# Three stretches put in program order, w_out's words kept in PSUM, key and query copies moved from VectorE to ScalarE

## The chip, the cores and the metric

The kernel runs on one NeuronCore of a Trainium2 chip. Its engines are named as the profile names them: PE (TensorE, with PEld its weight loads), DVE (VectorE), ACT (ScalarE), POOL (GpSimd) and SP (SyncE, which here only issues transfers). The metric is the device time of one execution in microseconds (us); the median of three runs is compared.

## The reference

Three layers follow each other on 4 sequences of 576 tokens, 8 heads of 64.

```python
# 1 attention with a decay
scores = q @ k.T / 8 + cum[:, None] - cum[None, :]      # cum = cumsum(log(clip(f)))
x = softmax(causal(scores)) @ v                          # -> x: 2304 tokens x 512
# 2 dense layer
h = x @ w_in                                             # 512 -> 2048
x = (h * clip(h + 3, 0, 6) / 6) @ w_out                  # 2048 -> 512
# 3 eight experts, one per token
e_idx = argmax(x @ w_gate); gate_w = softmax(x @ w_gate)[e_idx]
eom = sigmoid(x @ w_output_gate)[e_idx]
out = gate_w * eom * (relu(x @ w1[e_idx]) @ w2[e_idx])   # 512 -> 1024 -> 512
```

## The kernel before, in words

Every float32 operand is held as two 16-bit parts, a high part (`hi`, float16, written by ACT) and the rest (`lo`, bfloat16, by DVE or POOL), and each product is three matmuls (hi by hi, hi by lo, lo by hi).

**Attention** runs per sequence `b` through units. `("q", b, h, qbs)` is one head's query blocks: `score` (PE line 288, then DVE line 335, which adds the mask and takes the row minimum into `nm`), `soft` (ACT exponential, line 369; then a transpose of the weights, on PE for the first units, by DMA later) and `pv` (PE lines 421 to 423, after every second head DVE lines 444 to 446 into `xs`, ACT 449 and POOL 450 into `xn`). The PSUM tile `pv` has one buffer. `("p", b, n)` prepares a piece of K and Q: the first four pieces by PE transposes (lines 225 to 230), the later ones by DMA transposes, after which DVE copies one half of K into `K2` (line 246) and one half of Q into `Q2` (line 269). `plan` lists the units; for sequence 0 the pieces 2 and 3 stand after `AT2` and `AT3` units of the first group. `decay` computes `cum` on ACT and DVE, `setup` fills masks and constants on POOL.

**The dense layer** works on chunks `c` of 384 tokens. `moe1_steps(c)` does 16 steps of 12 matmuls (line 688), each evacuated by ACT (692), DVE (695), ACT (696) and DVE or POOL (700), with three PSUM buffers `mm`; then four groups of 48 matmuls with w_out (line 711). Chunk c can start when its tokens' `xn` have been transposed by DMA (`xtrans`, line 484, issued by SP).

**Weights of the dense layer** come as 64-bit floats. `conv_raw` turns one piece of 512 words a partition into float32 by three integer operations on DVE (lines 651, 653, 655; the intermediate `tp` is the PSUM tile `cv`, one buffer, the result `t` an SBUF tile `w32`, two buffers), then ACT writes `hi` (658) and POOL (for w_in) or DVE (for w_out) writes `lo` (659). There are 16 pieces of each matrix. w_in is converted before chunk 0, w_out while chunk 0 runs.

**Routing and experts.** `gate_steps` computes the gates of a chunk, `rank_onehot` (931) and `table` (909, 913 to 922) the lists of tokens per expert; `gather` (POOL 943, then a DMA transpose by SP, 946) fetches them. For experts 0 and 1 the first block of tokens (`blocks` (0,)) is taken from the first five chunks alone, gathered into `wi`, and multiplied (`expert1`, line 969, tile `wi`; `expert2`, line 988) before the remaining tokens' tables are needed. Then `round_` does everything else; it begins by loading the counts of the experts into registers of each engine (`values_load`, line 1183, eight TENSOR_LOADs an engine).

**Order.** A scheduler with a model of the engines orders most instructions by priority; inside `tc.manual_schedule(engines=...)` the listed engines keep the program's order. Before, that held for SP during the first part, and for PE, ACT and DVE inside `round_(True)` only. `tc.issue_after(ins)` keeps what is written inside it behind `ins` on that engine.

Of the kernel before, what the change touches and what calls it, by code (L numbers as in the profile page):

```python
# [18 lines left out]
P = 128  # L19
# [17 lines left out]
AT2, AT3 = 0, 4  # L37
# [21 lines left out]
def attention_moe_kernel(ctx: ExitStack, tc: tile.TileContext, q, k, v, f, w_in, w_out,  # L59
# [36 lines left out]
    def setup():  # L96
        nc.gpsimd.memset(ident, 1.0)
        nc.gpsimd.affine_select(out=ident, in_=ident, pattern=[[1, P]], compare_op=ALU.is_equal, fill=0.0, base=0,
                                channel_multiplier=-1)
        nc.gpsimd.memset(mask, 0.0)  # L100
        for c in range(2):
            ms_ = mask[c * 64:c * 64 + 64, 512:640]
            nc.gpsimd.affine_select(out=ms_, in_=ms_, pattern=[[-1, 128]], compare_op=ALU.is_ge, fill=-1e15,
                                    base=c, channel_multiplier=2)
        nc.gpsimd.memset(mask4, 0.0)
        for hf in range(2):
            nc.gpsimd.affine_select(out=mask4[hf * 64:hf * 64 + 64], in_=mask4[hf * 64:hf * 64 + 64],
                                    pattern=[[-1, 64]], compare_op=ALU.is_ge, fill=-1e15, base=0,
                                    channel_multiplier=1)
        nc.gpsimd.memset(bias3, 3.0)  # L110
        for t in Q2:
            nc.gpsimd.memset(t[64:67], PSC)
        for t in vt:
            nc.gpsimd.memset(t[:, :, :, 64:65], 1.0)

            nc.gpsimd.memset(t[64:128, 4, :, 65:129], 0.0)


    cumd = dram.tile([15, B * H, P], F16, name="cumd")

    def decay():
        ft = ap1.tile([P, 576], F32, tag="ms", name="ft", bufs=3)[0:B * H]
# [8 lines left out]
        nc.gpsimd.memset(cpt[:, :, S:640], 0.0)  # L131
        cp = cpt[:, :, 0:S]
# [6 lines left out]
        nc.vector.tensor_tensor(out=cp[:, 2], in0=ones, in1=cp[:, 1], op=ALU.subtract)  # L139
# [78 lines left out]
    def split_transposed(nm, i, hi, lo, copy):  # L218
# [3 lines left out]
        for c in range(2):  # L222
# [7 lines left out]
            nc.gpsimd.tensor_copy(out=copy[c], in_=hi[c])  # L230

    def prep_k(i):
# [13 lines left out]
        nc.vector.tensor_copy(out=k2[0:64], in_=k1[0:64])  # L246

    def prep_q(i):
# [20 lines left out]
        nc.vector.tensor_copy(out=q2[0:64, :, 0:r], in_=q1[64:128, :, 0:r])  # L269
# [280 lines left out]
    def attn_seq():  # L550
# [10 lines left out]
        with tc.high_priority(offset=ATTN_FIRST):  # L561
            cp = decay()
        setup()
        load(0, "kq")
        ahead(0)
        load(1, "kq")
        ahead(1)
        prep_k(0)
        prep_q(0)
        load(0, "v")  # L570
        store_decay(cp)
        ahead(2)
        load(1, "v")
        for hh in range(2):
            load_cum(0, hh)
        prep_k(1)
        prep_q(1)
# [62 lines left out]
    def conv_raw(nm, i):  # L640
# [3 lines left out]
        else:  # L644
# [4 lines left out]
        t = stp.tile([P, WL // 4], I32, tag="w32", name="w32", bufs=2)  # L649
        tp = ps_cv.tile([P, WL // 4], I32, tag="cv", name="cv")  # L650
        nc.vector.tensor_scalar(out=tp, in0=w[:, :, 1], scalar1=3, scalar2=0x3FFFFFFF,
                                op0=ALU.logical_shift_left, op1=ALU.bitwise_and)
        nc.vector.scalar_tensor_tensor(out=tp, in0=w[:, :, 1], scalar=-0x40000000, in1=tp, op0=ALU.bitwise_and,
                                       op1=ALU.bitwise_or)
        nc.vector.scalar_tensor_tensor(out=t, in0=w[:, :, 0], scalar=29, in1=tp, op0=ALU.logical_shift_right,
# [85 lines left out]
    def setup_gates():  # L741
# [5 lines left out]
        nc.gpsimd.memset(allone, 1.0)  # L747
# [263 lines left out]
    def ahead(i):  # L1011
        for _ in range(AHEAD[i]):
            load_next(nc.sync)
# [119 lines left out]
    count_rounds()  # L1133
    for i in range(NBL, NB):
        rank_onehot(R, i, P, CAP)
    table(R, P, const, ps_mm, (1, 2), NB)

    for e in range(2):
        for _ in expert1(e, ps_mm, (0,)):
            pass  # L1140
# [54 lines left out]
    ET = mybir.EngineType  # L1195
    with tc.manual_schedule(engines={ET.PE, ET.Activation, ET.DVE}):
        round_(True)
# [38 lines left out]
```

## Time and profile before

| | us |
|---|---|
| median of 3 runs | 835.37 (833.76 to 836.37) |
| the profiled execution, whole | 831.17 |
| its span, first to last instruction | 829.5 |
| PE busy in it | 746.0 (90%) |
| DVE busy | 486.3 (59%) |
| ACT busy | 427.3 (52%) |
| mean granted TensorE clock | 0.962 |

The profiled execution is 4.2 us (0.5%) below the median of the runs. Durations below come from it; a difference worked out from them is then applied to the median. A busy share is an average over stages that are limited by different engines, so stages are read one by one. [...]

### The profile page before, as it was taken

How to read it: one execution, taken by the hardware profiler on the slowest of the kernel's cores; microseconds unless marked ns; L12 is line 12 of the kernel's file. 1: busy time of each engine (PE TensorE's matmuls, PEld its weight loads, DVE VectorE, ACT ScalarE, POOL GpSimd, SP SyncE). 2: the span in 40 equal slices, each digit the busy share in tenths (PEclk: the TensorE clock that was granted, in tenths of full speed). 3: DMA queues.
4: the chain of work that ended last, by engine and by line, in shares of the span. 5: the costliest groups of instructions: out<-in, count | busy, mean ns of one | idle time of the engine just before them, and what ended most of it. 6: DMA issues, size and time to landing. Idle time of an engine off the chain costs nothing. (4 is left out here: it accounts for less than half of the span.)

```text
span 829.5 us, 16702 instructions
## 1 busy us (share of the span) xinstructions
PE 746.0 (90%) x6166; PEld 480.1 (58%) x6177; DVE 486.3 (59%) x1302; ACT 427.3 (52%) x879; POOL 314.1 (38%) x388
## 2 busy tenths in 40 slices
PE   4745998889899989998999999999889999999993
PEld 2533455545566645665665656666769665667641
DVE  7998999838852865158723777760313555554510
ACT  4864776557754774256733655550113555454510
POOL 9546777656744463256522500000131322210010
PEclk9986999979999999998999999999899999999997
DMA  8758789999995684479623847612463899795410
GB/s 247 218 184 190 173 186 236 214 129 164 174 169 115 137 153 83 72 119 168 109 50 71 144 130 237 187 41 51 78 147 86 249 275 276 221 266 206 149 39 28
DMA packets 263779, 127.96 MB, mean 154 GB/s; under 512 B 214658, under 2 KB 247522, under 8 KB 263684
## 3 DMA queue, kind: packets, MB, share of 16 engines
q1 hardware_dynamic: 251860, 105.20, 58.1%
q0 software_dynamic: 4960, 15.73, 5.6%
q10 hardware_dynamic: 6864, 5.80, 2.5%
q8 instruction: 54, 0.88, 0.5%
q14 instruction: 41, 0.34, 0.2%
HBM read 71.52 MB, written 10.08 MB: 98 GB/s over the span
## 5 line engine op out<-in xcount | busy, mean ns | idle before, releaser
L688 PE MATMUL mm<-xT,wi 128*128 128x384 f16 (+1 forms) x1152 | 211.9, 332 | 9.1 <-DMA xT<-xn 4.9
L711 PE MATMUL mm<-g,wo 128*128 128x384 f16 (+1 forms) x1152 | 201.8, 328 | 0.4 <-DVE hr L695 0.4
L688 PEld LDWEIGHTS <-wi 128*128 128x128 f16 (+1 forms) x1152 | 111.0, 99 | 88.8 <-issue 21.5
L711 PEld LDWEIGHTS <-wo 128*128 128x128 f16 (+1 forms) x1152 | 111.7, 98 | 74.4 <-issue 3.8
L969 PEld LDWEIGHTS <-W 128*128 128x128 f16 (+1 forms) x1344 | 102.8, 101 | 15.2 <-issue 6.8
L369 ACT ACTIVATE ms<-ms,nm 128x512 f32<-128x512 f32 (+4 forms) x144 | 79.5, 579 | 55.5 <-DVE nm L335 30.5
L872 DVE TENSOR_TENSOR W<-stw,W 128x1024 bf16<-128x1024 f32 x64 | 77.7, 1224 | 50.6 <-ACT W L871 50.2
L387 POOL TENSOR_TENSOR pn<-ms,pn 128x384 bf16<-128x384 f32 (+1 forms) x80 | 83.0, 1044 | 62.2 <-ACT pn L386 53.4
L969 PE MATMUL mm<-xs,W 128*128 128x256 f16 (+3 forms) x1152 | 96.8, 246 | 5.9 <-DMA xs<-xg 3.6
L988 PE MATMUL mm<-W,hT 128*128 128x512 f16 (+1 forms) x422 | 93.8, 379 | 1.1
L871 ACT ACTIVATE W<-stw 128x1024 f16<-128x1024 f32 x64 | 66.8, 1054 | 45.4 <-DMA stw<-in_moe_w_dram 42.9
L335 DVE CUSTOM_DVE_ANT_1 ms<-sc,mask 128x128 f32<-128x128 f32 (+3 forms) x128 | 58.9, 485 | 24.6 <-PE sc L288 13.9
L988 PEld LDWEIGHTS <-hT 128*128 128x128 f16 (+1 forms) x432 | 41.9, 98 | 50.9 <-issue 1.6
L696 ACT ACTIVATE g<-hr 128x384 f16<-128x384 f32 x96 | 49.9, 520 | 41.2 <-DVE hr L695 40.6
L700 DVE TENSOR_TENSOR g<-hr,g 128x384 bf16<-128x384 f32 x80 | 53.8, 673 | 25.7 <-ACT g L696 25.5
L695 DVE SCALAR_TENSOR_TENSOR hr<-hr,mm 128x384 f32<-128x384 f32 x96 | 52.6, 548 | 16.1 <-ACT hr L692 15.4
L973 DVE SCALAR_TENSOR_TENSOR hT<-mm,hT 128x128 bf16<-128x128 f32 (+1 forms) x96 | 32.6, 355 | 47.9 <-ACT hT L972 43.3
L288 PE MATMUL sc<-K,q 128*128 128x256 f16 (+3 forms) x192 | 49.1, 300 | 12.8 <-DVE nm L335 9.1
L692 ACT ACTIVATE hr<-mm,bias 128x384 f32<-128x384 f32 x96 | 54.5, 568 | 11.5 <-PE mm L688 10.1
L995 POOL DMA_INDIRECT out_dram<-y,ids x18 | 20.1, 1115 | 96.4 <-ACT y L994 56.1
L421 PE MATMUL pv<-vt,pt 128*128 128x65 f16 x320 | 42.0, 199 | 15.6 <-DVE xs L446 9.5
L943 POOL DMA_INDIRECT xg<-rows,ids x22 | 24.9, 1130 | 70.7 <-DMA xs<-xg 63.7
(186 smaller groups left out, 1128.3 us busy)
## 6 DMA issues: line engine op xcount, KB each, us to landing
stw<-in_moe_w_dram SPq DMA_DIRECT2D x64, 512.0 KB
wo<-in_moe_w_in_dram SPq DMA_DIRECT2D x16, 512.0 KB
raw<-in_moe_w_out_dram ACTq DMA_DIRECT2D x11, 512.0 KB
rows<-rw POOLq DMA_DIRECT2D x15, 256.0 KB, 4.0
ldk<-in_k_dram SPq DMA_DIRECT2D x14, 256.0 KB
ldq<-in_q_dram SPq DMA_DIRECT2D x14, 256.0 KB
ldv<-in_v_dram SPq DMA_DIRECT2D x13, 256.0 KB
g<-in_moe_w_out_dram SPq DMA_DIRECT2D x3, 512.0 KB
```

Of the source, the lines that this page charges most:

```text
L335: nc.vector.tensor_tensor_reduce(out=pairs(ms[:, off:off + w]), in0=ps[:, 0:w].rearrange("p (c j) -> p c j", c=2), in1=pairs(mask[:, 640 - ...
L369: nc.scalar.activation(out=ms[:, off:off + w], in_=ms[:, off:off + w], func=AF.Exp, scale=-1.0, bias=nm[:, i:i + 1])
L387: nc.gpsimd.tensor_tensor(out=lo.bitcast(BF16), in0=ms[:, 0:N], in1=hi, op=ALU.subtract)
L688: nc.tensor.matmul(ps[:, 0:w], lhsT=l.bitcast(BF16) if a else l, rhs=r.bitcast(BF16) if b2 else r, start=i == 0, stop=i == 3 * KD - 1)
L692: nc.scalar.activation(out=hr, in_=ps[:, 0:w], func=AF.Relu, bias=bias3)
L695: nc.vector.scalar_tensor_tensor(out=hr, in0=hr, scalar=6.0, in1=ps[:, 0:w], op0=ALU.min, op1=ALU.mult)
L700: either.tensor_tensor(out=g[:, m, 1, 0:w].bitcast(BF16), in0=hr, in1=g[:, m, 0, 0:w], op=ALU.subtract)
L711: nc.tensor.matmul(ps[:, 0:w], lhsT=l.bitcast(BF16) if a else l, rhs=r.bitcast(BF16) if b2 else r, start=i == 0, stop=i == 3 * NF - 1)
L871: nc.scalar.activation(out=hi, in_=sts[i], func=AF.Copy)
L872: nc.vector.tensor_tensor(out=lo.bitcast(BF16), in0=sts[i], in1=hi, op=ALU.subtract)
L969: nc.tensor.matmul(ps[:, 0:w], lhsT=l.bitcast(BF16) if a else l, rhs=r.bitcast(BF16) if b2 else r, start=i == 0, stop=i == 3 * KD - 1)
L988: nc.tensor.matmul(ps, lhsT=l.bitcast(BF16) if a else l, rhs=r.bitcast(BF16) if b2 else r, start=i == 0, stop=i == 3 * NF2 - 1)
```

## The change

The program's beginning (`decay`, the first loads and pieces 0 and 1) is put in program order on PE, ACT, DVE and POOL; `ident` is made first and the rest of `setup` inside `decay`. The constants for routing are written by POOL only behind the last copy of the split K and Q pieces (`hold[-1]`), and the first conversion of w_in behind the decay's last operation (`hold[0]`). Pieces 2 and 3 of sequence 0 move from places 0 and 4 to 3 and 6. The copies of lines 246 and 269 go from DVE to ACT. For w_out the converted words stay in the PSUM tile `cv`, in place. In routing, two steps of `expert1(0)` are written ahead of the remaining `rank_onehot` and `table`, and from there PE, ACT and DVE keep the program's order up to the end of `round_(True)`.

```diff
-AT2, AT3 = 0, 4
+AT2, AT3 = 3, 6
...
-    def setup():
+    def setup_ident():
         nc.gpsimd.memset(ident, 1.0)
         nc.gpsimd.affine_select(out=ident, in_=ident, pattern=[[1, P]], compare_op=ALU.is_equal, fill=0.0, base=0,
                                 channel_multiplier=-1)
+
+    def setup():
         nc.gpsimd.memset(mask, 0.0)
...
     def decay():
+        setup_ident()
...
         nc.gpsimd.memset(cpt[:, :, S:640], 0.0)
+        setup()
...
-        nc.vector.tensor_tensor(out=cp[:, 2], in0=ones, in1=cp[:, 1], op=ALU.subtract)
+        hold.append(nc.vector.tensor_tensor(out=cp[:, 2], in0=ones, in1=cp[:, 1], op=ALU.subtract).ins)
...
-            nc.gpsimd.tensor_copy(out=copy[c], in_=hi[c])
+            last = nc.gpsimd.tensor_copy(out=copy[c], in_=hi[c])
+        hold.append(last.ins)
...
-        nc.vector.tensor_copy(out=k2[0:64], in_=k1[0:64])
+        nc.scalar.activation(out=k2[0:64], in_=k1[0:64], func=AF.Copy)
...
-        nc.vector.tensor_copy(out=q2[0:64, :, 0:r], in_=q1[64:128, :, 0:r])
+        nc.scalar.activation(out=q2[0:64, :, 0:r], in_=q1[64:128, :, 0:r], func=AF.Copy)
...
-        with tc.high_priority(offset=ATTN_FIRST):
+        ET = mybir.EngineType
+        with tc.manual_schedule(engines={ET.PE, ET.Activation, ET.DVE, ET.Pool}):
             cp = decay()
...
-        t = stp.tile([P, WL // 4], I32, tag="w32", name="w32", bufs=2)
         tp = ps_cv.tile([P, WL // 4], I32, tag="cv", name="cv")
-        nc.vector.tensor_scalar(out=tp, in0=w[:, :, 1], scalar1=3, scalar2=0x3FFFFFFF,
-                                op0=ALU.logical_shift_left, op1=ALU.bitwise_and)
+        with tc.issue_after(hold[0]) if (nm, i) == ("wi", 0) else nullcontext():
+            nc.vector.tensor_scalar(out=tp, in0=w[:, :, 1], scalar1=3, scalar2=0x3FFFFFFF,
+                                    op0=ALU.logical_shift_left, op1=ALU.bitwise_and)
...
+        t = stp.tile([P, WL // 4], I32, tag="w32", name="w32", bufs=2) if nm == "wi" else tp
...
-        nc.gpsimd.memset(allone, 1.0)
+        with tc.issue_after(hold[-1]):
+            nc.gpsimd.memset(allone, 1.0)
+            setup_tables()
...
+    first = [expert1(e, ps_mm, (0,)) for e in range(2)]
+    manual = ctx.enter_context(ExitStack())
+    manual.enter_context(tc.manual_schedule(engines={ET.PE, ET.Activation, ET.DVE}))
+    run(first[0], 2)
     for i in range(NBL, NB):
         rank_onehot(R, i, P, CAP)
     table(R, P, const, ps_mm, (1, 2), NB)
-
-    for e in range(2):
-        for _ in expert1(e, ps_mm, (0,)):
-            pass
+    for g_ in first:
+        run(g_, F2 // P)
...
-    with tc.manual_schedule(engines={ET.PE, ET.Activation, ET.DVE}):
-        round_(True)
+    round_(True)
+    manual.close()
```

What this does to the engines' orders is shown at three places. In the changed program the lines stand 5 to 16 further down (225 is 230, 335 is 341, 651 is 657, 659 is 667, 969 is 981, 972 is 984, 988 is 1000, 994 is 1006, 1183 is 1199).

ACT at the end of the experts' first block; `wi<-mm` are evacuations of `expert1` on that block, `wi<-mm,cf` of its `expert2`, `hT<-mm` those of `round_`. Before:

```order
L972 ACTIVATE wi<-mm 128x128 x15
L1183 TENSOR_LOAD cnt x8
L972 ACTIVATE hT<-mm 128x128
L972 ACTIVATE wi<-mm 128x128
L994 ACTIVATE wi<-mm,cf 128x512 x2
L972 ACTIVATE hT<-mm 128x128 x7
```

And changed:

```order
L984 ACTIVATE wi<-mm 128x128 x16
L1006 ACTIVATE wi<-mm,cf 128x512 x2
L1199 TENSOR_LOAD cnt x8
L984 ACTIVATE hT<-mm 128x128 x8
```

The eight register loads moved from inside the first product of that block to behind its second product.

PE around its eight register loads; `wi` marks the first block, `xs` the tokens that `round_` gathers. Before:

```order
L969 MATMUL mm<-wi,W_7248 128x128
L969 LDWEIGHTS W_7129
L1183 TENSOR_LOAD cnt x8
L969 MATMUL mm<-xs_8461,W_7129 128x128
```

And changed:

```order
L1000 MATMUL mm<-W_7640,wi 128x512
L981 LDWEIGHTS W_7116
L1199 TENSOR_LOAD cnt x8
L981 MATMUL mm<-xs_8448,W_7116 128x128
```

Before, 144 of the 192 matmuls of line 969 on the first block stand ahead of the loads, and behind them the other 48, mixed with twenty on `xs`, and then the 48 of line 988; changed, all 192 and the 48 of line 988 stand ahead of the loads and nothing on `xs` does.

DVE at the very beginning; `ft`, `ones` and `cp` belong to `decay`, lines 651, 653 and 655 to the conversion of w_in, 229 to the split of K and Q. Before:

```order
L136 CAST cp<-ones 32x576
L651 TENSOR_SCALAR cv<-wo 128x512
L137 TENSOR_TENSOR ones<-ones,cp 32x576
L653 SCALAR_TENSOR_TENSOR cv<-wo,cv 128x512
L138 CAST cp<-ones 32x576
L655 SCALAR_TENSOR_TENSOR w_280<-wo,cv 128x512
L139 TENSOR_TENSOR cp<-ones,cp 32x576
L229 TENSOR_TENSOR K_93<-mm,K_93 64x512
```

And changed:

```order
L141 CAST cp<-ones 32x576
L142 TENSOR_TENSOR ones<-ones,cp 32x576
L143 CAST cp<-ones 32x576
L144 TENSOR_TENSOR cp<-ones,cp 32x576
L234 TENSOR_TENSOR K_93<-mm,K_93 64x512 x2
L234 TENSOR_TENSOR q_184<-mm,Q_0_88 64x8x64
L657 TENSOR_SCALAR cv<-wo 128x512
```

The first conversion moved from among the decay's operations to behind the first three splits.

## Rows read from the trace of the kernel before

**Rows 1.** The page: busy time of each engine in the whole span, then the granted TensorE clock in 40 equal slices, in tenths.

```profile
PE 746.0 (90%) x6166; PEld 480.1 (58%) x6177; DVE 486.3 (59%) x1302; ACT 427.3 (52%) x879; POOL 314.1 (38%) x388
PEclk9986999979999999998999999999899999999997
```

**Rows 2.** Stretches of the span (us): their length, then busy us of PE, PEld, DVE, ACT, POOL with their instruction counts, granted clock, DMA share and GB/s.

```profile
0.00:68.00 68.00, 37.65 (x324) 26.66 (x324) 60.80 (x156) 42.69 (x90) 43.31 (x78) 0.89 0.76 219
73.00:160.00 87.00, 76.85 (x583) 46.25 (x583) 81.44 (x189) 59.40 (x125) 63.35 (x65) 0.97 0.93 203
160.00:200.00 40.00, 35.85 (x350) 21.51 (x347) 20.54 (x69) 24.33 (x54) 22.59 (x31) 0.85 0.91 145
200.00:400.00 200.00, 190.10 (x1617) 119.17 (x1614) 119.81 (x401) 117.22 (x266) 99.26 (x121) 0.98 0.73 133
```

**Rows 3.** What PE waited for from 73 to 560 us: us in total, times, longest.

```profile
PE sc L288 <- DVE nm L335: 7.0, 9, 1.3
PE mm L688 <- DVE hr L695: 3.4, 6, 1.0
PE pv L421 <- DVE xs L446: 2.3, 1, 2.3
PE pv L421 <- DVE xs L462: 2.2, 4, 1.3
PE sc L288 <- DMA q<-qp: 1.5, 1, 1.5
```

**Rows 4.** The timeline of the first 24 us: start, us, engine, line, operation, and in brackets the idle time before it and what ended it.

```profile
7.26 2.77 PE L225 MATMUL mm<-ident,g 128*64 128x128 f32 x12 [7.26 <-POOL ident L98]
8.35 0.69 DVE L651 TENSOR_SCALAR cv<-wo 128x512 int32<-128x512 int32 x1 [0.84 <-DMA wo<-in_moe_w_in_dram]
12.02 0.69 DVE L229 TENSOR_TENSOR K<-mm,K 64x512 f16<-64x512 f32 x1
23.04 0.29 DVE L335 CUSTOM_DVE_ANT_1 ms<-sc,mask 128x128 f32<-128x128 f32 x1
```

**Rows 5.** The timeline where the dense layer's first chunk starts: the last evacuation of attention that it needs, its transpose, its first matmuls.

```profile
67.77 0.28 DVE L446 TENSOR_TENSOR xs<-pv,rl 128x128 f32<-128x128 f32 x1
70.17 1.26 SPq L484 DMA_TRANSPOSE xT<-xn  x1
73.37 5.91 PE L688 MATMUL mm<-xT,wi 128*128 128x384 f16 x26 [3.72 <-DMA xT<-xn]
```

**Rows 6.** Durations: the instructions of lines 659 and 246 (ns minimum/median/maximum, first and last start), groups by form (busy us, mean ns), then two stretches with DVE's busy time in line 246 alone and the same two in line 269 alone.

```profile
L659 DVE TENSOR_TENSOR wo<-w,wo x16: 669/778/2959, 80.2 to 158.0; 128x512 bf16<-128x512 f32 x16
L659 DVE TENSOR_TENSOR wo<-w,wo 128x512 bf16<-128x512 f32 x16 | 18.0, 1127 | 0.1
L229 DVE TENSOR_TENSOR K<-mm,K 64x512 f16<-64x512 f32 x8 | 5.5, 682 | 0.3 <-ACT K L228 0.2
L246 DVE COPY K<-K x12: 412/419/1374, 99.3 to 368.7; 64x1024 f16<-64x1024 f16 x12
73.00:160.00 87.00, 4.08 (x6) 0.97 0.93 203
160.00:400.00 240.00, 5.64 (x10) 0.96 0.76 135
73.00:160.00 87.00, 5.23 (x6) 0.97 0.93 203
160.00:400.00 240.00, 5.38 (x10) 0.96 0.76 135
L871 ACT ACTIVATE W<-stw 128x1024 f16<-128x1024 f32 x64 | 66.8, 1054 | 45.4 <-DMA stw<-in_moe_w_dram 42.9 <-SPq L1200 1.9 <-ACTq L1172 0.3
L658 ACT ACTIVATE wo<-w 128x512 f16<-128x512 f32 x16 | 10.0, 624 | 4.6 <-DVE w L655 4.5
```

**Rows 7.** PE's timeline in routing, from the first block's first product to the first product of `round_`.

```profile
593.72 2.74 PE L969 MATMUL mm<-wi,W 128*128 128x128 f16 x24
596.26 1.19 PE L909 MATMUL mm<-M,R 128*128 128x56 bf16 x21
597.26 7.56 PE L969 MATMUL mm<-wi,W 128*128 128x128 f16 x120
608.38 0.72 PE L969 MATMUL mm<-xs,W 128*128 128x128 f16 x10 [3.55 <-DMA xs<-xg]
613.80 10.52 PE L988 MATMUL mm<-W,wi 128*128 128x512 f16 x47
624.16 8.04 PE L969 MATMUL mm<-xs,W 128*128 128x128 f16 x141
```

**Rows 8.** The register loads of line 1183 on PE's and ACT's sequencers (ns minimum/median/maximum, first and last start), and the branch of line 1191 with the matmuls written ahead of it.

```profile
L1183 PEldq TENSOR_LOAD <-cnt x8: 298/314/755, 603.7 to 607.2; - x8
L1183 ACTq TENSOR_LOAD <-cnt x8: 274/285/748, 612.8 to 616.1; - x8
L1191 PEldq COMPARE_BRANCH  x12: 65/172/326, 645.8 to 811.9; - x12
644.48 10.52 PE L988 MATMUL mm<-W,hT 128*128 128x512 f16 x47
```

**Rows 9.** Two stretches behind a gap of PE, columns as in rows 2.

```profile
180.00:185.00 5.00, 3.79 (x30) 2.09 (x30) 1.85 (x7) 2.42 (x6) 2.56 (x4) 0.50 0.88 134
610.00:611.00 1.00, 1.00 (x12) 1.00 (x10) 0.29 (x1) 0.28 (x1) 0.69 (x2) 0.50 0.44 55
```

More of the change, by code (lines that the diff above doesn't have):

```diff
@@ L116, in setup @@
             nc.gpsimd.memset(t[64:128, 4, :, 65:129], 0.0)
+    hold = []
     cumd = dram.tile([15, B * H, P], F16, name="cumd")
     def decay():
+        setup_ident()
         ft = ap1.tile([P, 576], F32, tag="ms", name="ft", bufs=3)[0:B * H]
@@ L560, in attn_seq @@
         unsoft = []
-        with tc.high_priority(offset=ATTN_FIRST):
+        ET = mybir.EngineType
+        with tc.manual_schedule(engines={ET.PE, ET.Activation, ET.DVE, ET.Pool}):
             cp = decay()
[L563 to L577, printed above, removed]
+            load(0, "kq")
+            ahead(0)
+            load(1, "kq")
+            ahead(1)
+            load(0, "v")
+            store_decay(cp)
+            ahead(2)
+            for hh in range(2):
+                load_cum(0, hh)
+            load(1, "v")
+            prep_k(0)
+            prep_q(0)
+            prep_k(1)
+            prep_q(1)
         load(2, "kq")
@@ L746, in setup_gates, with setup_tables @@
         nc.vector.tensor_tensor(out=wg[:, 1].bitcast(BF16), in0=wg32, in1=wg[:, 0], op=ALU.subtract)
-        nc.gpsimd.memset(allone, 1.0)
+        with tc.issue_after(hold[-1]):
+            nc.gpsimd.memset(allone, 1.0)
+            setup_tables()
+    def setup_tables():
         nc.gpsimd.affine_select(out=tri, in_=allone, pattern=[[1, P]], compare_op=ALU.is_gt, fill=0.0, base=0,
@@ L1133, in attention_moe_kernel @@
     count_rounds()
+    ET = mybir.EngineType
+    first = [expert1(e, ps_mm, (0,)) for e in range(2)]
+    manual = ctx.enter_context(ExitStack())
+    manual.enter_context(tc.manual_schedule(engines={ET.PE, ET.Activation, ET.DVE}))
+    run(first[0], 2)
     for i in range(NBL, NB):
@@ L1193, in round_ @@
                     pass
-    ET = mybir.EngineType
-    with tc.manual_schedule(engines={ET.PE, ET.Activation, ET.DVE}):
-        round_(True)
+    round_(True)
+    manual.close()
     more = nc.values_load(nrounds[0:1, 0:1], min_val=0, max_val=NT // CAP)
```

## Prediction

> **What bounds the kernel now.** I read the page first: PE is busy 90% of the span [rows 1], so the time is PE's work plus its gaps plus what a low granted clock costs; the clock row shows slices well below 9. A busy share of the whole span hides the stages, so the next view is the table of stretches [rows 2]. From 0 to 68 us PE is busy 37.65 of 68 us and DVE 60.80: here DVE is the limit. From 73 to 160 us, while the dense layer's first chunk runs and w_out is converted, PE is busy 76.85 of 87 and DVE 81.44 (94%): PE has the work, DVE makes the gaps. From 200 to 400 DVE falls to 60% and PE is at 95%. The chain of waits of PE [rows 3] names the enders from 73 to 560 us: four rows ended by DVE hold 7.0 + 3.4 + 2.3 + 2.2 = 14.9 us, DMA of q 1.5. Last comes routing, read from PE's timeline [rows 7]: a gap of 3.55 us ahead of the first matmul on `xs`, and 5.42 us (608.38 to 613.80) for the 68 matmuls behind it, which at the later pace (8.04 us for 141, so 57 ns) are 3.9.
>
> **The beginning.** Removed: the decay's operations wait once for w_in's first words (DVE idle 0.84 us [rows 4]) because a conversion stands among them. In program order the decay ends at about 12.02 - 0.84 - 3 x 0.69 = 9.1 us, and the splits follow at once if PE has transposed. PE waited until 7.26 us for `ident` [rows 4], which is now POOL's first work, so it has. The routing constants leave POOL's start; POOL was not what DVE waited for, so that is nothing, and 14 short operations later on POOL (63.35 of 87 us busy [rows 2]) are hidden under its free 23 us. Scores begin earlier (DVE's first at 23.04 us [rows 4]; with two splits and four conversion operations fewer ahead of it, about 6 x 0.69 = 4 us). But nearly all of DVE's work is still ahead of the evacuation at 67.77 us that releases the first chunk [rows 5]: in the changed order only two conversion operations fewer (2 x 0.69 = 1.4 us). With 0.6 of the 0.84 that is **2.0 us**; lower bound 0, upper 5 (all of DVE's free time before 68 us but the first 2.8 us that it waits for its input: 68 - 60.80 - 2.8 = 4.4, plus part of the 1.4). What follows the evacuation, the transpose at 70.17 and the first matmul at 73.37 [rows 5], moves with it.
>
> **The copies to ScalarE.** They took DVE 4.08 + 5.23 = 9.3 us from 73 to 160 us and 5.64 + 5.38 = 11.0 us from 160 to 400 [rows 6]. On ACT a copy of 1024 elements is not in the trace; the nearest rows are 1.054 us for 1024 elements with float32 input and 0.624 for 512 [rows 6]. I take 1.05 for the 24 long and 0.62 for the 8 short ones, 30 us in all, 10.9 of it (8 long, 4 short) from 73 to 160 us, where ACT is busy 59.40 of 87: it goes to 81%. That is covered, as long as ACT is not held in front of a copy.
> The undisturbed copy took DVE 0.41 us [rows 6], so each result is some 0.64 us later than it could be. [...] By rows the loss is small: PE waited for q once [rows 3], so one such delay, 0.6 us.
>
> **w_out's words in PSUM.** The last subtraction took 1.127 us in the mean, 0.669 at best and 2.959 at worst [rows 6]. From PSUM it is not in the trace; the nearest row is line 229, the same operation with one input in PSUM, 0.682 us, at times when POOL was busy too. So 16 x (1.127 - 0.682) = 7.1 us of DVE, all before 160 us; bounds 0 and 7.3 (all at 0.669). [...]
> Added: `cv` has one buffer, so the next conversion waits for ACT's copy (0.624 [rows 6]) and DVE's own subtraction, and the subtraction itself waits behind ACT. Before, idle time at that line was 0.1 us [rows 6], because other conversions filled it. In the changed order about half of the 16 subtractions have next to nothing between them and line 655. Bounds 0 and 16 x 0.62 = 10 us of DVE; I take 8 x 0.5 = 4. Queued behind a waiting subtraction is line 695, for which PE waited 3.4 us in all [rows 3].
>
> **What that is worth to PE.** From 73 to 160 us DVE is relieved of 9.3 + 7.1 - 4 = 12.4 of 81.4 us, later of 11.0. PE's waits ended by DVE are 14.9 us. I take 40% of them, **6 us**. Bounds: 0 if DVE's waits merely move, and 14.9 plus a stretch at half clock if they all go. [...]
>
> **Routing.** Before, the 3.55 us gap has two causes that end close together: the eight register loads on PE's sequencer (603.7 to 607.2 + 0.3 [rows 8]) and the gathered tokens (608.38 [rows 7]). Changed, 48 more matmuls on `wi` and the 48 of line 988 stand ahead of both. From 593.72: 24 matmuls 2.74 us to 596.5; 36 of line 909 at 1.19/21 = 57 ns, 2.05, and an estimated 0.5 for the last `rank_onehot`, which now stand behind two evacuations, to 599.0; 168 at 57 ns, 9.6, to 608.6, no earlier than the tokens come; 48 at 10.52/47 = 224 ns [rows 7], 10.7, to 619.3; the 20 on `xs` that were already done before, 1.1, to 620.4. Before this point was 624.16 [rows 7]: 3.7 us less.
> PE's loads, 3.8 us, must fit under line 988. The branch at 645.8 [rows 8] stands behind 24 matmuls that began at 644.48 and need 24 x 0.224 = 5.4 us, to 649.9: the sequencer was 4 us ahead of the array. So I count nothing, with 3.8 as the other bound. ACT's loads take 612.8 to 616.4 [rows 8]; they lay under line 988 and now stand behind its last evacuation, so ACT is free at about 619.3 + 3.7 = 623.0. PE fills five PSUM buffers meanwhile (5 x 12 x 57 ns = 3.4, to 622.7) and waits until ACT and DVE release one, about 0.9 us. So **2.8 us**, bounds 0 and 4.5. It carries to the end, since PE stays busy there.
>
> **Sum.** 2.0 + 6 + 2.8 = 10.8 us. The profiled execution's 831.17 becomes 820.4; it lies 4.2 under the median of the runs, so 835.4 - 10.8 = 824.6 for the median, some **824.5**.
>
> **Rivals.**
> [...]
> *The one buffer eats the relief:* each of 16 conversions stalls DVE 0.6 us and the middle gains nothing: 835.4 - 4.8 = 830.6. For it: DVE has no spare room there; against it: it needs the full bound.
> *No change:* PE's loads stay exposed (3.8), the beginning gains nothing, the middle about 1: 834.5. Against it: the sequencer's 4 us of lead.
> *Slower:* ACT keeps its order, so a copy that stands ahead of its DMA transpose holds the line 692 behind it, and with it PE's three PSUM buffers. A hold that PE cannot bridge is priced like the one in the rows: 2.3 us of gap [rows 3] and 2.5 of half clock behind it [rows 9], 4.8 together. One leaves the sum below zero even with the middle's gain gone; from two on, 9.6 - 4.8 = +4.8 us, the kernel is slower: 840.2. Against it: DVE bore the same waits ahead of line 695, and PE's longest wait for that line was 1.0 us [rows 3].
>
> **How the numbers follow.** This kernel's runs spread 0.3%; that is about what can be told from no change (832.9 to 837.9). Chances: the forecast 0.48 (its own range 818 to 831), larger gain 0.14, eaten relief 0.18, no change 0.10, slower 0.10. Faster: 0.46 + 0.14 + 0.14 + 0.02 = 0.76; same 0.02 + 0.04 + 0.06 = 0.12; slower the rest, 0.12. Leaving out the slowest case and the far end of the larger gain gives 811 to 837.
>
> **What would show it.** Routing: no gap ahead of the first matmul on `xs`, PE's register loads inside line 988, a gap of about 1 us some five steps into `round_`. Beginning: first DVE score at 18 to 19 us, first matmul of line 688 at 71 to 72. Middle: line 659's counterpart at 0.68 us each without spread; DVE below 85% from 71 to 158 us; PE's waits ended by DVE near 9 us. The prediction is wrong if waits ended by ACT appear on line 688, if the first chunk's second half waits for w_out, or if a new stretch of half clock opens between 80 and 560 us.

## The result and the profile after

The changed kernel is slower: **844.24 us** in the median of four runs (843.33 to 845.02) against 834.57 for the kernel before (four runs, 833.55 to 836.37), a ratio of **1.0121, 95% interval 1.0097 to 1.0145**. (The ratios in this text are those on record with their intervals; they need not be the quotient of two medians, which is 1.0116 here.) The forecast was 824.5 with a range of 811 to 837.

Two rows of its page, busy time of each engine and the granted clock in 40 slices, answer to [rows 1]:

```profile
PE 752.1 (89%) x6177; PEld 482.5 (57%) x6177; DVE 467.2 (55%) x1270; ACT 451.2 (54%) x911; POOL 308.7 (37%) x388
PEclk9775999959999999998999999999999999999997
```

The span is 843.2 us, 13.7 more than before. PE's busy time grew by 752.1 - 746.0 = 6.1 us with the same work, that is by matmuls at a lower clock (0.943 in the mean against 0.962), and its idle time by the other 7.6. DVE lost 19 us of work, ACT gained 24. The ninth slice of the clock row (169 to 190 us) is a 5 where a 7 stood, and the second to fourth (21 to 84 us) are 7, 7, 5 where 9, 8, 6 stood.

The same stretches as in [rows 2], same columns (length, then PE, PEld, DVE, ACT, POOL busy, granted clock, DMA share, GB/s):

```profile
0.00:68.00 68.00, 38.02 (x324) 29.49 (x324) 59.85 (x150) 42.32 (x88) 41.87 (x77) 0.80 0.69 206
73.00:160.00 87.00, 76.12 (x598) 44.87 (x596) 58.93 (x165) 68.20 (x138) 61.13 (x69) 0.93 0.96 192
160.00:200.00 40.00, 30.58 (x224) 17.00 (x225) 25.51 (x74) 25.60 (x54) 24.25 (x32) 0.66 1.03 186
200.00:400.00 200.00, 187.65 (x1586) 116.81 (x1585) 105.76 (x359) 119.94 (x256) 85.02 (x103) 0.97 0.65 121
```

From 73 to 160 us DVE went from 81.44 busy us to 58.93, and PE got nothing from it: 76.12 against 76.85. From 160 to 200 PE does less, at a clock of 0.66 instead of 0.85.

How far behind the kernel is can be read where a chunk of the dense layer starts. The first matmuls of chunks 0 and 1 in the changed kernel, then that of chunk 1 before (chunk 0 stands in [rows 5], 73.37):

```profile
75.60 7.11 PE L696 MATMUL mm<-xT,wi 128*128 128x384 f16 x26 [2.10 <-DMA xT<-xn]
198.80 1.46 PE L696 MATMUL mm<-xT,wi 128*128 128x384 f16 x8
```

```profile
182.25 2.10 PE L688 MATMUL mm<-xT,wi 128*128 128x384 f16 x6 [1.21 <-DMA xT<-xn]
```

It is 2.2 us behind at chunk 0 and 16.5 at chunk 1. At the gates of the last chunk it is 16.8 behind (605.66 against 588.89), at the end 13.7. So everything is lost by 200 us, and routing gives 3.1 back. From chunk 0's first matmul to chunk 1's PE is busy 105.0 of 123.2 us, before 94.95 of 108.9. Its idle time there grew by 4.3 us only; the rest of the lag is work at a lower clock (0.85 against 0.94) and some fifty more matmuls that the scheduler put there.

What PE waited for from 73 to 560 us, as in [rows 3] (line 719 is the second product, 666 ACT's `hi` of the weights, 452 and 468 the evacuations of `pv`):

```profile
PE pv L427 <- DMA pt<-pn: 9.8, 3, 5.2
PE pv L427 <- DVE xs L468: 5.9, 4, 4.9
PE pv L427 <- DVE xs L452: 5.7, 4, 3.4
PE mm L719 <- ACT wo L666: 5.4, 3, 4.1
PE mm L696 <- DVE hr L703: 3.1, 4, 1.1
PE sc L294 <- DVE nm L341: 3.1, 4, 1.4
```

The wait for the row minimum `nm` fell from 7.0 to 3.1, as DVE's relief would have it, but the evacuations take 5.9 + 5.7 where they took 2.2 + 2.3, so the four rows that DVE ends hold 17.8 us instead of 14.9 (the prediction looked for 9). [rows 3] leaves out some rows of the same view, among them two more that DVE ends (2.6 and 2.0 us); with all of them DVE ends 20.3 us of PE's waiting before and 20.9 after, so DVE's relief took nothing off it. The first row, PE waiting for softmax weights `pt` that a DMA transposes, grew too (in all its rows from 1.5 to 11.1 us), but it does not go with the loss: undo_copies below, a faster kernel, has 11.1 as well. New is the fourth row: chunk 0's second product waits for w_out, which the prediction had named as a sign that it is wrong. The reason stands in DVE's group of the last subtraction (busy, mean ns, then the idle time in front of it):

```profile
L667 DVE TENSOR_TENSOR wo<-cv,wo 128x512 bf16<-128x512 f32 x16 | 11.0, 687 | 14.3 <-ACT wo L666 14.3
```

The subtraction itself is as short as forecast, but DVE stands 14.3 us in front of it, at nine of the sixteen. The two longest are shown, first from 154 to 160 us. The timeline, with the idle time before a row in brackets:

```profile
154.29 0.69 DVE L663 SCALAR_TENSOR_TENSOR cv<-raw,cv 128x512 int32<-128x512 int32 x1
155.84 0.64 ACT L316 ACTIVATE vt<-ldv 128x512 f16<-128x512 f32 x1 [3.97 <-DMA ldv<-in_v_dram]
157.07 0.63 ACT L275 ACTIVATE Q<-q 64x512 f16<-64x512 f16 x1 [0.60 <-DMA q<-qp]
158.66 0.57 ACT L666 ACTIVATE wo<-cv 128x512 f16<-128x512 f32 x1
159.27 0.69 DVE L667 TENSOR_TENSOR wo<-cv,wo 128x512 bf16<-128x512 f32 x1 [3.62 <-ACT wo L666]
159.29 0.50 PE L719 MATMUL mm<-g,wo 128*128 128x384 f16 x2 [4.05 <-ACT wo L666]
```

The words are ready at 155.0. ACT stands behind a load of V and then behind a query copy that waits for its transpose, and comes to `wo` at 158.66; DVE stands for 3.62 us, and PE for 4.05: PE waits here for the high part itself, which ACT writes, not for DVE. Then from 164 to 172 us:

```profile
169.36 0.52 ACT L392 ACTIVATE pn<-ms 128x384 f16<-128x384 f32 x1 [3.63 <-DMA pt<-pn]
170.29 0.58 ACT L666 ACTIVATE wo<-cv 128x512 f16<-128x512 f32 x1
170.90 0.69 DVE L667 TENSOR_TENSOR wo<-cv,wo 128x512 bf16<-128x512 f32 x1 [2.56 <-ACT wo L666]
171.51 0.41 DVE L452 TENSOR_TENSOR xs<-pv,rl 128x256 f32<-128x256 f32 x1
172.07 0.21 PE L427 MATMUL pv<-vt,pt 128*128 128x65 f16 x1 [3.37 <-DVE xs L452]
```

Here PE waits for an evacuation that has nothing to do with w_out: it is queued on DVE behind the standing subtraction. What held ACT was a buffer of softmax weights (`pn`) that a transpose still read. A key or query copy stands shortly ahead of ACT's `wo` in three of the nine places (at 127.17, 139.63 and 157.07 us), so how the copies make ACT late is shown only in part. Behind these gaps the clock is low:

```profile
170.00:190.00 20.00, 12.45 (x102) 6.70 (x103) 15.76 (x45) 14.55 (x31) 12.48 (x16) 0.50 1.01 201
```

For these 20 us the granted clock is 0.50; the matmuls of `pv` start 0.054 us apart there (172.10 to 172.75 us), and 0.031 apart at 163.14 to 163.67, where it is 0.99. Before, the clock averages 0.66 from 175 to 190 us, by estimate from that mean about 10 us at 0.50 around [rows 9].

### The profile page after: what moved, and what is told of

Its sections match the earlier page's. It is cut to its first block, busy times and chain, and to the rows that moved or that the text cites. A ratio compares the mean times of both kernels' runs of the same rounds, so it can differ in the third digit from the quotient of the medians.

```text
span 843.2 us, 16728 instructions
## 1 busy us (share of the span) xinstructions
PE 752.1 (89%) x6177; PEld 482.5 (57%) x6177; DVE 467.2 (55%) x1270; ACT 451.2 (54%) x911; POOL 308.7 (37%) x388
## 5 line engine op out<-in xcount | busy, mean ns | idle before, releaser
L696 PE MATMUL mm<-xT,wi 128*128 128x384 f16 (+1 forms) x1152 | 214.6, 334 | 5.5 <-DVE hr L703 3.1
L696 PEld LDWEIGHTS <-wi 128*128 128x128 f16 (+1 forms) x1152 | 111.8, 100 | 85.4 <-issue 20.3
L981 PEld LDWEIGHTS <-W 128*128 128x128 f16 (+1 forms) x1344 | 100.4, 98 | 13.5 <-issue 6.0
L708 DVE TENSOR_TENSOR g<-hr,g 128x384 bf16<-128x384 f32 x80 | 59.2, 741 | 26.7 <-ACT g L704 26.5
L427 PE MATMUL pv<-vt,pt 128*128 128x65 f16 x320 | 44.1, 201 | 31.0 <-DVE xs L452 13.9
L729 DVE SCALAR_TENSOR_TENSOR x<-mm,x 128x384 bf16<-128x384 f32 x24 | 13.2, 555 | 76.9 <-ACT x L728 76.9
```

Source lines behind the costliest of these rows:

```text
L696: nc.tensor.matmul(ps[:, 0:w], lhsT=l.bitcast(BF16) if a else l, rhs=r.bitcast(BF16) if b2 else r, start=i == 0, stop=i == 3 * KD - 1)
L708: either.tensor_tensor(out=g[:, m, 1, 0:w].bitcast(BF16), in0=hr, in1=g[:, m, 0, 0:w], op=ALU.subtract)
L981: nc.tensor.matmul(ps[:, 0:w], lhsT=l.bitcast(BF16) if a else l, rhs=r.bitcast(BF16) if b2 else r, start=i == 0, stop=i == 3 * KD - 1)
```

## Experiments

The kernel before ran between 828.6 and 842.0 us in these comparisons, so each ratio to it is known to 0.2 to 0.5%. Its medians in them were 833.1 to 836.1 us, so ratios are compared and not us. S stands for the beginning with its later places, C for the copies on ACT, W for w_out's words in PSUM, R for routing. Many runs are such sets, and this is what they gave (in brackets the label):

| | without W | with W |
|---|---|---|
| before alone | 1 | 1.0013 (alone_words) |
| R | 0.9949 (alone_routing) | 0.9943 (words_routing) |
| S, R | 1.0011 (begin_routing) | 0.9966 (undo_copies) |
| C, R | 1.0020 (copies_routing) | 1.0116 (undo_begin) |
| S, C, R | 0.9922 (undo_words) | **1.0121 (the change)** |
| S with places 0 and 4, C, R | 1.0045 (csr_at04) | 1.0116 (full_at04) |
| C | 1.0078 (alone_copies) | |
| S | 1.0066 (alone_begin) | |

**Each part alone, from the kernel before.** alone_words:

```diff
-        t = stp.tile([P, WL // 4], I32, tag="w32", name="w32", bufs=2)
         tp = ps_cv.tile([P, WL // 4], I32, tag="cv", name="cv")
+        t = stp.tile([P, WL // 4], I32, tag="w32", name="w32", bufs=2) if nm == "wi" else tp
```

> The kernel before with one edit: w_out's words stay in the one PSUM buffer cv. Theory 'chain' (the conversions of w_out now follow each other through one buffer, three DVE operations, ACT's copy, DVE's subtraction, so the last of them ends near 188 us instead of near 159, and chunk 0's second product waits for it): this edit alone carries most of the loss, 834.6 + 8 to 14 us, 843 to 849, with waits of the second product on ACT's wo and the last subtraction behind 170 us. Theory 'ScalarE' (the copies make ACT late, and the conversion is late only because it waits for ACT): without the copies this edit is harmless, 830 to 836, last subtraction before 165 us.

Measured: 1.0013 (0.9985 to 1.0042). The last subtraction starts at 177.4 us, as 'chain' has it, yet the time hardly moves, as 'ScalarE' has it: by itself the chain through `cv` makes the conversion late and does no harm that can be told.

alone_copies:

```diff
-        nc.vector.tensor_copy(out=k2[0:64], in_=k1[0:64])
+        nc.scalar.activation(out=k2[0:64], in_=k1[0:64], func=AF.Copy)
...
-        nc.vector.tensor_copy(out=q2[0:64, :, 0:r], in_=q1[64:128, :, 0:r])
+        nc.scalar.activation(out=q2[0:64, :, 0:r], in_=q1[64:128, :, 0:r], func=AF.Copy)
```

> The kernel before with one edit: the key and query copies on ACT. Theory 'chain': DVE's relief is kept and nothing waits, 830 to 835. Theory 'ScalarE' (ACT, in order, is held by copies behind their transposes and is full at some places): 840 to 846, with PE waits ended by ACT from 73 to 260 us.

Measured: 1.0078 (1.0044 to 1.0112), 842.6 us. ACT's groups of the two lines from 73 to 560 us:

```profile
L269 ACT ACTIVATE Q<-q 64x1024 f16<-64x1024 f16 x12 | 12.7, 1055 | 7.6 <-DMA q<-qp 7.4
L246 ACT ACTIVATE K<-K 64x1024 f16<-64x1024 f16 x12 | 12.6, 1049 | 7.8 <-DMA K<-kp 7.7
```

The durations are those forecast; in front of the long copies ACT stands for 7.4 + 7.7 = 15.1 us until their transposes have landed. Time is lost by the copies, but PE's waits ended by ACT, which the theory named, did not come. Nor does this standing tell a slow kernel from a fast one: copies_routing has 15.0 us of it at 1.0020, and undo_words, the fastest with these copies, 10.9.

alone_begin and alone_routing are the diff's parts for the beginning and for routing, shown cut:

```diff
-AT2, AT3 = 0, 4
+AT2, AT3 = 3, 6
...
-        with tc.high_priority(offset=ATTN_FIRST):
+        with tc.manual_schedule(engines={ET.PE, ET.Activation, ET.DVE, ET.Pool}):
             cp = decay()
...
```

> The kernel before with one edit: the beginning in program order, with routing's tables moved back and pieces 2 and 3 of the first sequence at places 3 and 6. In the changed kernel the first chunk starts at 75.60 us where it started at 73.37 before. Theory 'chain': that is all it costs, 834.6 + 2.2, about 837. Theory 'beginning' (the order of the start disturbs the order of everything behind it, and the half-clock stretch at 20 to 30 us lets the start fall behind): 842 to 848. The prediction's step would be 832.6.

Measured: 1.0066 (1.0040 to 1.0092), 841.4 us; between the two theories, and on the other side of the prediction's step.

```diff
+    manual.enter_context(tc.manual_schedule(engines={ET.PE, ET.Activation, ET.DVE}))
+    run(first[0], 2)
     for i in range(NBL, NB):
         rank_onehot(R, i, P, CAP)
...
```

> The kernel before with one edit: routing in program order. From the first product on the experts' first block to the end of its second product with twenty matmuls on xs done, the changed kernel's trace shows 27.0 us where before's shows 30.4. So every theory says 834.6 - 3.4 = about 831.2, and the order ahead of routing unchanged. If it is 834 or more, the gain shown there was given back later.

Measured: 0.9949 (0.9926 to 0.9973), 4.3 us less; 3.4 was expected, and the interval (2.3 to 6.2) holds it.

The four parts alone add up to 0.13 + 0.78 + 0.66 - 0.51 = 1.06%, close to the 1.21% of the whole. That looked like an answer, and the next runs took it away.

**One part undone, from the changed kernel.** undo_words is the diff of alone_words the other way round:

> The changed kernel with w_out's words back in the SBUF tile. Alone, that edit moved the time by 0.13% (alone_words), though it let w_out's conversion end at 177.4 us instead of 158.0. Theory 'parts add up': undoing it gives 844 - 1 = 843, a ratio to before of about 1.010. Theory 'chain needs company' (one buffer does harm only where ACT is also held by the copies, so that the first chunk's second half waits 5.4 us for wo and falls to half clock from 170 to 190 us): undoing it gives 12 of the 16.5 us back that stand at chunk 1's start, 830 to 835, ratio 0.995 to 1.001.

Measured: **0.9922 (0.9889 to 0.9955), 826.0 us.** The part that costs 0.13% alone is worth 2% here. The trace has no wait of line 719 on `wo`, chunk 1 starts at 181.67 us, and the last subtraction at 156.8:

```profile
L667 DVE TENSOR_TENSOR wo<-w,wo x16: 669/685/2510, 84.2 to 156.8; 128x512 bf16<-128x512 f32 x16
  ACT wo L666: 2.9, 4
```

(Minimum, median and maximum in ns, first and last start; below it the idle time ahead that ACT ended, and how often.) DVE stands 2.9 us where it stood 14.3.

undo_copies, the copies back on DVE:

> The changed kernel with the key and query copies back on DVE. Alone, that edit cost 0.78%. Theory 'parts add up': 844 - 6.5 = 837.7, ratio about 1.004. Theory 'chain needs company': the waits on wo go, more than the part alone comes back, 829 to 834, ratio 0.994 to 0.999. If the copies were DVE's relief that the rest lives on: 846 or more.

Measured: 0.9966 (0.9942 to 0.9989), 831.3 us, 1.5% less than the changed kernel; the words are still in `cv` and the last subtraction starts at 181.8, but DVE stands only 4.3 us in front of all sixteen. The conversion's late end is not what costs.

undo_begin, the old beginning with places 0 and 4:

> The changed kernel with the old beginning (the scheduler's order, pieces 2 and 3 at places 0 and 4, routing's tables at the start); copies on ACT, words in PSUM and routing in program order stay. Alone, the beginning cost 0.66%. Theory 'parts add up': 844 - 5.5 = 838.5, ratio about 1.005. Theory 'the middle has its own fault' (copies and words delay chunk 1 whatever the start): 841 to 845.

Measured: 1.0116 (1.0074 to 1.0158), 843.5 us, nothing gained. The fault lies in the middle, whatever the beginning.

**The standing itself.** hi_on_dve lets DVE write w_out's high part, so that the subtraction waits for no other engine, while the words stay in the one buffer:

```diff
-        last_act.append(nc.scalar.activation(out=hi, in_=tf, func=AF.Copy).ins)
+        if nm == "wo":
+            nc.vector.tensor_copy(out=hi, in_=tf)
+        else:
+            last_act.append(nc.scalar.activation(out=hi, in_=tf, func=AF.Copy).ins)
```

> The changed kernel, with w_out's high part written by DVE instead of ACT; the words stay in the one buffer cv, copies, beginning and routing as changed. So every use of cv is on DVE and the subtraction waits for nobody. DVE gets 16 more operations, about 16 x 0.65 = 10.4 us, and loses its 14.3 us of waiting for ACT's wo. Theory 'subtraction behind ACT' (the loss is DVE standing at the subtraction until ACT comes to wo, behind copies and loads): last subtraction before 168 us, no wait of the second product on wo, ratio to before 0.990 to 1.000. Theory 'order' (it is only that the scheduler makes another order of everything, good or bad by chance): no reason to get better than 1.005.

Measured: 0.9969 (0.9942 to 0.9995), 829.7 us, 1.5% less than the changed kernel. The group of the subtraction:

```profile
L670 DVE TENSOR_TENSOR wo<-cv,wo 128x512 bf16<-128x512 f32 x16 | 11.0, 687 | 0.2
```

DVE has 11 us more work and no standing, PE never waits for `wo`, and the loss is gone. One number of the expectation missed: the last subtraction starts at 177.8, not before 168. So again the end of the conversion is not the cost; ACT's part in it is. The edit does three things at once, though: it ends DVE's standing, it ends PE's own waits for the high part, and it takes sixteen copies (9.3 us) off ACT. And one thing it does not end: the low clock. Its stretch from 160 to 200 us, and below it that of undo_copies:

```profile
160.00:200.00 40.00, 32.12 (x255) 18.12 (x255) 24.55 (x74) 21.80 (x48) 20.18 (x27) 0.72 0.91 160
160.00:200.00 40.00, 29.17 (x243) 16.85 (x240) 25.31 (x73) 23.65 (x53) 22.61 (x31) 0.79 0.98 188
```

In hi_on_dve the granted clock is 0.50 from 160 to 180 us (PE busy 12.1 of 20), in undo_copies from 171 to 187, and in alone_words (1.0013) from 163 to 183; their means from 160 to 200 us, 0.79 and 0.74, fit that. So a stretch of 16 us and more at a granted clock of 0.50 stands in kernels with the words in PSUM that lost nothing as well, and does not by itself account for the loss.

one_sbuf goes back to SBUF words, but with one buffer:

```diff
-        t = stp.tile([P, WL // 4], I32, tag="w32", name="w32", bufs=2) if nm == "wi" else tp
+        if nm == "wo" and not one:
+            one.append(stp.tile([P, WL // 4], I32, tag="w32", name="w32", bufs=2))
+        t = one[0] if nm == "wo" else stp.tile([P, WL // 4], I32, tag="w32", name="w32", bufs=2)
```

> The changed kernel with w_out's words back in SBUF (0.992 of before in undo_words), but in one buffer instead of two. The first two operations of the next conversion, which write cv, can run ahead; the third waits for the subtraction. If one buffer as such is the fault: ratio 1.003 to 1.012 and the last subtraction behind 170 us. If the fault is that nothing of the next conversion can run while DVE stands at the subtraction: 0.990 to 0.997, last subtraction before 165 us.

Measured: 1.0018 (0.9985 to 1.0051), 835.8 us, between the two. DVE stands only 2.8 us for ACT, but the subtractions take 1.321 us in the mean with two SBUF inputs. With the standing nearly gone, 1.0 of the 2.0% that undo_words gained came back. Not decisive.

**Sets that tell the interplay.** begin_routing and copies_routing are the change without C and W, and without S and W:

> The changed kernel without the copies on ACT and without the words in PSUM: the beginning and routing alone. By the single parts (1.0066 and 0.9949) the sum is 1.0015; with the words as well (undo_copies) it was 0.9966. If the beginning costs 5.5 us by its own mechanism wherever it stands: 1.000 to 1.004. If what the beginning costs depends on the order behind it: 0.993 to 0.997.

> The kernel before with the copies on ACT and routing in program order; old beginning, words in SBUF. By the single parts 1.0078 and 0.9949 the sum is 1.0027. It is undo_begin (1.0116) without the words in PSUM. If the words do their harm together with the copies whatever the beginning: 0.995 to 1.003 here, at least 8 us less than undo_begin. If the harm needs the new beginning: 1.008 or more.

Measured: 1.0011 (0.9987 to 1.0035) and 1.0020 (0.9990 to 1.0050); both as the single parts say. Beside undo_words, which has both, this leaves a puzzle: S and C cost 0.6 and 0.7% each and together nothing that can be told (0.9922 against 0.9949, whose intervals overlap).

nocopy_r and nocopy_sr leave the key and query copies of sequences 1 to 3 out of the computation, at no engine's cost, from alone_routing and begin_routing:

```diff
-        nc.vector.tensor_copy(out=k2[0:64], in_=k1[0:64])
+        if i < 5:
+            nc.vector.tensor_copy(out=k2[0:64], in_=k1[0:64])
...
```

> Old beginning, words in SBUF, routing in program order (alone_routing, 0.9949), with the key and query copies of sequences 1 to 3 left out of the computation: what DVE's relief is worth if it costs no other engine anything. With the copies on ACT this order gave 1.0020. If relief is worth something here and ACT's load is what costs: 0.985 to 0.990. If DVE's relief is worth nothing with the old beginning: 0.993 to 0.997. If it is only the order that each edit makes anew: anything, 0.995 to 1.003 too.

> New beginning, words in SBUF, routing in program order (begin_routing, 1.0011), with the same copies left out. With the copies on ACT it gave 0.9922. If the new beginning puts more on DVE behind 73 us, so that relief is worth more there: 0.980 to 0.991, at least 1% below begin_routing. If relief is worth as little as it would seem with the old beginning and undo_words was a lucky order: 0.997 to 1.003.

Measured: 0.9862 (0.9830 to 0.9894) and 0.9896 (0.9861 to 0.9931). DVE's relief is worth 0.9% and 1.15%, 7.3 and 9.6 us, with either beginning. What ACT's carrying costs against that is 1.0020 - 0.9862 = 1.6% with the old beginning and 0.9922 - 0.9896 = 0.3% with the new.

at36 changes the places alone, in the kernel before; csr_at04 and full_at04 put them back in undo_words and in the whole change:

```diff
-AT2, AT3 = 0, 4
+AT2, AT3 = 3, 6
```

> The kernel before with one edit: pieces 2 and 3 of the first sequence at places 3 and 6. In the eight traces with the new beginning and these places the first chunk starts at 74.65 to 75.60 us, in the others at 72.00 to 74.24, and with the new beginning at the old places (begin_at04) at 72.90. If the places are what delays it: first chunk behind 74.5 us, ratio 1.002 to 1.008. If the program order of the start does it: 72 to 74, ratio 0.997 to 1.002.

Measured: 1.0010 (0.9991 to 1.0029). The first matmuls of chunks 0 and 1:

```profile
75.19 3.04 PE L688 MATMUL mm<-xT,wi 128*128 128x384 f16 x9 [3.32 <-DMA xT<-xn]
181.41 3.06 PE L688 MATMUL mm<-xT,wi 128*128 128x384 f16 x9 [1.04 <-DMA xT<-xn]
```

The places do delay the first chunk, by 1.8 us, and it costs nothing: chunk 1 starts 0.8 us earlier than in the kernel before.

begin_at04 has the new beginning with the old places:

> The kernel before with the new beginning, but pieces 2 and 3 of the first sequence left at places 0 and 4. It parts the program order of the start from the later places of the pieces. If the places cost the 5.5 us that the whole edit costs alone (841 there), this is 834 to 836, ratio 1.000; if the order of the start does it (waits of 4.4 and 5.0 us on PE ahead of 23 us, then half clock to 30), it stays at 839 to 842, ratio 1.005 to 1.008.

Measured: 1.0043 (1.0015 to 1.0071), between both.

> The best kernel so far (undo_words, 0.9922: new beginning, copies on ACT, words in SBUF, routing) with pieces 2 and 3 at the old places 0 and 4. If the later places are only a loss of some 2 us at the first chunk's start: 0.988 to 0.991. If the gain of the copies needs the later places: 0.996 to 1.003. If the order behind is chance: between.

Measured: 1.0045 (1.0016 to 1.0073), above every range that was expected; its interval reaches into the second alone (the gain of the copies needs the later places). It is 1.2% slower than undo_words by the same places that did nothing in at36.

> The whole change with pieces 2 and 3 at the old places 0 and 4: csr_at04 (1.0045) with w_out's words in PSUM. If the words cost 1% or more wherever ACT has the copies: 1.012 to 1.022, with DVE standing 8 us or more ahead of the last subtraction. If the loss in the changed kernel was chance of its order: 0.998 to 1.008.

Measured: 1.0116 (1.0070 to 1.0163), 844.0 us, 0.7% more than csr_at04; a little under what was expected, and above the bound set for chance of the order. PE waits for `wo` again, and DVE stands again:

```profile
PE mm L719 <- ACT wo L666: 3.7, 2, 2.5
L667 DVE TENSOR_TENSOR wo<-cv,wo 128x512 bf16<-128x512 f32 x16 | 11.0, 688 | 15.0 <-ACT wo L666 14.9
```

words_routing is alone_routing with the words in PSUM:

> The kernel before with w_out's words in PSUM and routing in program order, copies on DVE, old beginning: alone_routing (0.9949) with the words. If the words cost nothing where ACT has no copies: 0.993 to 0.999. If they cost 1% by themselves: 1.003 to 1.007.

Measured: 0.9943 (0.9915 to 0.9972), the same as without the words.

**What follows.** Read the table by rows. With the copies on DVE, W moves the time by +0.13, -0.06 and -0.45%, and DVE stands 8.1, 5.5 and 4.3 us for ACT. With the copies on ACT it costs 0.96, 2.0 and 0.7%, and DVE stands 9.9, 14.3 and 14.9 us. Three orders agree on each side, and hi_on_dve removes the standing and with it the loss while W and C both stay. Each of these kernels has an order of its own, so a single difference may carry some 1% of chance (csr_at04); the sign does not rest on one. That W does its harm together with C, and that the harm goes when ACT has no part in w_out's conversion, is shown so far. That the path is DVE standing behind ACT, and what is queued behind it, fits these rows and the place at 172 us, but no run isolates it: PE's own waits for the high part are another path in the changed kernel and in full_at04 (5.4 and 3.7 us), though not in undo_begin, which has none and lost 0.96% all the same; and ACT's load is a third. How much a standing costs is not shown either: the 8.1 us of alone_words cost nothing and the 9.9 of undo_begin 0.96%. The fastest version is undo_words (0.9922); routing alone (0.9949) lies inside its interval, and csr_at04 shows that a small change of places takes its gain away.

## Why the prediction was wrong

**Words in PSUM, the step that failed.** The duration was right: 0.687 us each, 0.693 at most, against 0.682 forecast, with POOL busy 61.13 of 87 us from 73 to 160 us. With the words in SBUF single ones took up to 2.959 us before [rows 6] and up to 4.365 in one_sbuf; what makes those long, no run isolates. The term for the one buffer was mis-sized: 4 us, at most 10; measured 14.3. The bound took ACT's copy at its own 0.62 us and added no time that ACT needs to come to it, though ACT's order has loads, transposes and now the copies in it. And the term was counted as DVE's busy time, of which there was plenty (58.93 of 87 us). What it cost was order: each of sixteen subtractions can stop the evacuations of `pv` and the row minima queued behind it, as at 172 us (3.37 us of PE), and PE itself waits where ACT's high part is late, as at 159 us (4.05 us). Undoing this one step brought 2.0% back.

**The copies.** Durations (1.055 and 0.627 us on ACT) and ACT's load (68.20 of 87 us, 78%; forecast 81%) were right. "Covered, as long as ACT is not held in front of a copy" was the condition, and it did not hold: 15.1 us of standing in alone_copies. It did not hold in undo_words either (10.9 us), where the copies cost nothing, so the standing alone is not the reason for the 0.7 to 0.8% that they cost with the old beginning. The relief of DVE did pay (7.3 and 9.6 us in nocopy_r and nocopy_sr), but not its taker.

**The worth of DVE's relief.** 6 us was forecast for copies and words together, and the relief by the copies alone is worth 7.3 to 9.6 where no engine takes them. The size was sound, if low; the reading under it was not complete, since [rows 3] leaves rows out and all waits ended by DVE were 20.3 us, not 14.9. In the changed kernel nothing of that worth reached PE: these waits are 20.9.

**The beginning.** Forecast: decay ends at 9.1, first score on DVE at 18 to 19, first chunk at 71 to 72 us. The trace:

```profile
4.44 2.74 PE L230 MATMUL mm<-ident,g 128*64 128x128 f32 x12 [4.44 <-POOL bias L112]
6.54 1.01 DVE L140 COPY ones<-ft 32x64 f32<-32x64 f32 x1
10.82 1.28 DVE L234 TENSOR_TENSOR K<-mm,K 64x512 f16<-64x512 f32 x2
11.56 3.62 PE L230 MATMUL mm<-ident,g 128*64 128x128 f32 x16 [4.38 <-DVE K L234]
20.63 0.28 DVE L341 CUSTOM_DVE_ANT_1 ms<-sc,mask 128x128 f32<-128x128 f32 x1
```

PE begins 2.8 us earlier, and then waits 4.38 for the splits, because they stand behind the whole decay, which ends at 10.78. In the eight traces with the new beginning and its places the first chunk starts at 74.65 to 75.60 us, 75.27 in the mean; in the eight of the old at 72.00 to 74.24, 73.27. So 2 us later instead of 2 earlier. The prediction never priced the later places, and at36 shows that they do it without any new order (75.19). The order at the old places gave 72.90, 73.65 and once 75.72 us (begin_at04, full_at04, csr_at04), so it gains little at best. at36 also shows that the first chunk's start does not carry to the end, which the step assumed.

**Routing, right.** The rows below are the first block's first product, its second product, the tokens of `round_` behind it, and PE's and ACT's register loads (ns, first and last start):

```profile
609.85 2.41 PE L981 MATMUL mm<-wi,W 128*128 128x128 f16 x24
625.13 10.52 PE L1000 MATMUL mm<-W,wi 128*128 128x512 f16 x48 [0.66 <-ACT wi L984]
635.65 19.36 PE L981 MATMUL mm<-xs,W 128*128 128x128 f16 x336
L1199 PEldq TENSOR_LOAD <-cnt x8: 306/310/942, 631.6 to 634.7; - x8
L1199 ACTq TENSOR_LOAD <-cnt x8: 274/276/505, 635.7 to 638.2; - x8
```

No gap stands ahead of `xs` any more, PE's loads lie inside line 1000, and from the first product to twenty matmuls on `xs` it takes 635.65 + 1.1 - 609.85 = 26.9 us where it took 30.4 [rows 7]: 3.5 against 3.7 forecast. The gap of 0.9 us behind ACT's loads did not come, so the whole 3.5 is kept.

**The sum and the rivals.** Without the words the prediction's own sum would be 2.0 + 6 x 9.3/12.4 + 2.8 = 9.3 us; undo_words measured 0.78%, 6.5. With them the outcome is beyond the slower rival (840.2 at a chance of 0.10). That rival held ACT behind a copy and priced a hold at 4.8 us, 2.5 of it for half a clock over 5 us; PE was busy for 3.79 of these [rows 9], so by estimate 1.9 at most. What came is its neighbour: ACT is held by a copy, a load or a transpose, and DVE is held behind ACT. The larger gain (chance 0.14) and the low end of the range need nearly all of the 14.9 us of DVE's waits to go, and a stretch at half clock with them; no run shows that term, and in the changed kernel these waits, all counted, went from 20.3 to 20.9 us and the clock stood at 0.50 from 170 to 190 us. The rival on the one buffer saw DVE stall but let only the middle's gain be lost. It had no half clock behind its stalls: from 170 to 190 us PE is busy 12.45 us at half clock, so by estimate up to 6.2 us of them are the clock's. A new stretch of half clock was named as a sign that the prediction is wrong, and it came; but hi_on_dve has one as long and is no slower than before, so it is not what parts the two.

**Open.** Why C gains 0.9% with the new beginning and its places, and costs 0.7% with the old. The relief is about the same in both (0.9 and 1.15%), which points to ACT's side; but two pieces moved by three places changed that set by 1.2% (csr_at04) and the kernel before by 0.1% (at36). The scheduler makes another order for each, and which wait in it decides was not found. By which path ACT's lateness costs PE its time in the changed kernel is open in part, as said above.

## What to carry to other kernels

A buffer released through a second engine cost here what that engine had queued ahead, its waits for transfers included (3.62 us of DVE at 159 us, behind ACT's load of V and query copy), and on the first engine what was queued behind (3.37 us of PE at 172 us), or nothing, as the 8.1 us of alone_words: price both queues, not the operation. Where a scheduler makes the order anew, a part that is harmless alone may cost 2% with another part, and single-part runs that add up to the right total can still name the wrong part; undo parts from the whole as well.

## What the runs showed of the hardware

A copy of 64 x 1024 float16 elements takes ACT 1.055 us, as long as 1024 elements with float32 input (1.054 [rows 6]); DVE did it in 0.419, the median [rows 6]. DVE's copy of 32 x 64 float32 elements in the decay takes 1.01 us in the row above, at a time when POOL fills `Q`; before, it took 0.26, and mainly by this stretch and three smaller ones the decay ends 1.7 us later than forecast. POOL was filling a tile beside the 0.26 us copy too (6.50 to 6.87 us), and what made the later one longer, no run here isolates. From PSUM instead of SBUF ACT's copy of 512 elements is a little shorter, 0.579 us against 0.624 [rows 6].
